# The last batch's q taken first and sorted by one-hots in its own layout: a linear attention with routed experts on one core

## The chip, the core and the metric

The kernel runs on one core of a Trainium2 chip. The metric is device time in microseconds (us), of one execution from its start to its end. The core has five engines with a queue of instructions each: TensorE (PE in the profile, PEld for its weight loads), VectorE (DVE), ScalarE (ACT), GpSimd (POOL) and SyncE (SP). An instruction waits for semaphores at the head of its queue, and what stands behind it waits too. SP issues the input transfers, POOL those of the experts' weights and of the output.

## The reference

The inputs are q, k and v of 8 batches, 8 heads, 576 positions and 64 features, one token number for each of the 4608 positions, and two weight matrices for each of 8 experts.

```
q_s = softmax(q) over the 64 features;  k_s = softmax(k) over the 576 positions
kv  = einsum('bhsd,bhse->bhde', k_s, v)
x   = einsum('bhsd,bhde->bhse', q_s, kv)         # as 4608 rows of 512
expert = token_ids * 2654435761 % 8
out[expert == e] = relu(x[expert == e] @ w1[e]) @ w2[e]     # w1: 512 x 1024, w2: 1024 x 512
```

## The kernel before, in words

The work has two stages. The first goes through the 8 batches (the loop at L750) and computes attention; while it does so it sorts the tokens of a batch by their expert and copies them into one tile xT, in which each expert has a stretch of 720 columns. The second goes through the experts: layer 1 (L692), ReLU, layer 2 (L717), and a store of the rows to their places (L733).

A batch of q, k or v lies in SBUF with 128 partitions: head parity times 64, and within a head 9 positions to a partition. There are two buffers each, so the loads of batch b + 2 are issued in batch b, once the tile is free (L776, L777); batches 0 and 1 are loaded ahead of the loop. q's load waits for exp_q, k's for exp_k, v's for cast_v of two batches before.

Within a batch b the order is written by hand, and each engine takes its own instructions in this order. ScalarE takes the exponentials of k (exp_k, L518); TensorE transposes the exponentials of q (transpose_q, L532); VectorE and ScalarE bring them to SBUF (qT_out, L544 to L547). TensorE then sorts the batch before: sort (L610) multiplies the attention's rows xn with a one-hot matrix, 384 columns for the first three tiles of 128 tokens and 192 for the other two, and ScalarE evicts to xs (L617). VectorE casts v to bf16 (cast_v, L526) and makes the one-hot matrix of a batch (one_hot, L601). kv (L557) multiplies k and v over 64 rows at a time, in pairs, into banks 6 and 7 of PSUM. kv_norm (L564, L568) divides by k's sum; qsum (L578, L582) has the sums of q's exponentials; attend (L586) multiplies, and VectorE scales the result to xn (L591). POOL copies 16 pieces of the sorted batch before to the experts' stretches (segments, L654).

Batch 0 has positions (L364 to L369), which gives each token its place, and segment_table (L373 and on); batch 2 has overflow (L402 and on).

At the seam of the stages the order on POOL is this. In batch 6 come 8 pieces of batch 5, then the four transfers of expert 0's w1 (weights1_half, L677, which wait until k of batch 7 has landed), then 8 more pieces. In batch 7 come the transfers of expert 1's w1 (weights1, L669) and expert 0's w2 (weights2, L683), then the pieces of batch 6 for experts 4 to 7. After the loop VectorE copies pieces for experts 0 to 3, and TensorE starts layer 1 of expert 0 on the first 320 columns, which need the pieces of batches 0 to 5 alone, with the sort of batch 7 between the second and the third of its four units (L821 to L825). Then expert 1 follows on its first 320 columns (L861). Layer 1 takes units of 256 hidden features (8 matmuls).

Of the kernel before, what the change touches and what calls it, by code (L numbers as in the profile page):

```python
# [4 lines left out]
F32 = mybir.dt.float32  # L5
# [159 lines left out]
def fused_kernel(nc, q, k, v, moe_token_ids, moe_w1, moe_w2, out):  # L165
# [4 lines left out]
    NC = 9  # L170
# [48 lines left out]
    selA = at("selA", [128, B * T, 128], BF16, vx0)  # L219
    selB = at("selB", [128, NG * TG, 2, B * T], BF16, vx0 + 10240)  # L220

    w1b, w2b, wreg = [], [], [qkv0, qkv0 + 18432, qkv0 + 36864, exp0]
    for i, o in enumerate(wreg):
        w1b.append(at("w1b%d" % i, [128, 4, F], BF16, o))
# [39 lines left out]
    dsf = at("dsf", [128, 4, NJ], F32)  # L264
    idxf = at("idxf", [128, B * T], F32)
    idx = at("idx", [128, B * T], I32)
    rk = [at("rk%d" % i, [128, 4], F32) for i in range(2)]
    rq = [at("rq%d" % i, [128, T, 8], F32) for i in range(2)]
    assert cur[0] <= 229000, cur[0]
# [8 lines left out]
    def dv(fn, R=(), W=(), P=()):  # L278
        em.op("dve", fn, R, W, P)
# [8 lines left out]
    b_q, b_k = [Buf(), Buf()], [Buf(), Buf()]  # L288
    b_v = [[Buf(), Buf()] for _ in range(2)]
    QKV = {"q": (qf, q), "k": (kf, k), "v": (vf, v)}  # L290

    def load_one(nm, b, p, js=range(2)):
        dst, src = QKV[nm]
        bb = [b_q[p]] if nm == "q" else [b_k[p]] if nm == "k" else [b_v[p][j] for j in js]
        js = slice(js[0], 4, 2 // len(js))
        em.dma("sync", "d_%s%d_%d" % (nm, p, js.start if js.step == 2 else 2), lambda e: e.dma_start(  # L296
            dst[p][:, js, :, :].rearrange("p h c d -> p h (c d)"),
            src[b].rearrange("(a h) (p c) d -> (h p) a (c d)", h=2, p=64)[:, js, :]), W=bb)

    load_one("q", 0, 0)  # L300
    em.dma("sync", "d_tok", lambda e: e.dma_start(
        tok64[:], moe_token_ids.rearrange("(b p c) -> p b c", b=B, p=64, c=NC)), P=[b_tok])
    b_vx = [[Buf(), Buf()] for _ in range(2)]
# [202 lines left out]
    def load(b, p):  # L506
        load_one("k", b, p)
        for js in ([(0,), (1,)] if b == B - 1 else [(0, 1)]):
            load_one("v", b, p, js)
# [11 lines left out]
            ACTF.Exp),  # L521
           R=[b_k[p]], W=[b_ek[p][j] for j in js])

    def cast_v(p, js=range(2)):
        o = slice(js[0], 4, 2 // len(js))
        dv(lambda e: e.tensor_copy(out=vx[p][:, o, :, 0:DH], in_=vf[p][:, o, :, :]), R=[b_v[p][j] for j in js],  # L526
           W=[b_vx[p][j] for j in js])

    def transpose_q(p):

# [17 lines left out]
                                   in_=PBH[:, 2048:2304].rearrange("p (j h x) -> p j h x", h=2, x=64)),  # L548
           R=[bk[2]], W=[b_qT[p][2]])

    def kv(p, js=range(2)):
        fns = []
        for j in js:
            for c in range(NC):
                for h2 in range(2):
                    r = slice(64 * h2, 64 * h2 + 64)
                    fns.append(lambda e, j=j, c=c, h2=h2, r=r: e.matmul(  # L557
                        PB[:, 6 + h2, 130 * j:130 * j + 130], ek[p][r, j, c, :, :].rearrange("p a d -> p (a d)"),
                        vx[p][r, j::2, c, :], start=(c == 0), stop=(c == NC - 1)))
        em.op("pe", fns, R=[b_ek[p][j] for j in js] + [b_vx[p][j] for j in js], W=[bk[6], bk[7]])  # L560

    def kv_norm(p):
        KV = PB[:, 6:8, 0:260].rearrange("p h (j a x) -> p j h a x", j=2, a=2)
        dv(lambda e: e.reciprocal(out=rk[p][:].rearrange("p (j h) -> p j h", h=2), in_=KV[:, :, :, 0, 64]),  # L564
           R=[bk[6], bk[7]], W=[b_rk[p]])
        for a in range(2):
            r = slice(64 * a, 64 * a + 64)
            dv(lambda e, a=a, r=r: e.tensor_tensor(  # L568
                out=kvn[p][r, :, a, :].rearrange("p (j h) x -> p j h x", h=2), in0=KV[r, :, :, a, 0:DH],
                in1=rk[p][r, :].rearrange("p (j h) -> p j h", h=2).unsqueeze(3).to_broadcast([64, 2, 2, DH]),  # L570
                op=ALU.mult), R=[bk[6], bk[7], b_rk[p]], W=([b_kvn[p]] if a == 0 else ()),
               P=(() if a == 0 else [b_kvn[p]]))

    def qt(p, t, j, h2):
        return qT[p][:, j, h2, 128 * t:128 * t + 128]
# [163 lines left out]
    def run(gen, n=2 * E):  # L739
        for _ in range(n):  # L740
            if next(gen, 0) == 0:
                break

    load(0, 0)
    load_one("q", 1, 1)
    load(1, 1)
    clear()
    exp_q(0, 0)
    exp_q(0, 1)
    for b in range(B):  # L750
        p = b % 2
        last = b == B - 1
        if last:
            transpose_q(p)
            exp_k(p, (0,))
            qT_out(p)
            exp_k(p, (1,))
            sort(1 - p, 0, 3)
            for j in range(2):
                cast_v(p, (j,))  # L760
                kv(p, (j,))
            sort(1 - p, 2, 0)
        else:
            exp_k(p)
            transpose_q(p)
            qT_out(p)
            if b > 0:
                sort(1 - p, 0, 3)
                sort(1 - p, 2, 0)
            if 1 < b < 6:  # L770
                load_segments(B - 2 + b // 4, "dve", 0, (b % 2,))
            cast_v(p)
            if b == 0:
                positions()
# [242 lines left out]
```

## Time and profile before

| what | us |
| --- | --- |
| median of three runs | 226.52 (226.42 to 226.86) |
| profiled execution | 226.57 |
| its span | 224.8 |
| PE busy | 192.4 (86%) |
| DVE busy | 124.2 (55%) |
| POOL busy | 117.8 (52%) |
| ACT busy | 106.8 (47%) |

The mean granted clock of TensorE was 0.982. In the page's slices each digit is the busy share of 5.62 us in tenths. A line of a chain or of a timeline begins with the start and the duration in us; "xN" is the number of instructions that it merges, and brackets at its end hold the idle time before it and what ended it. "DMA to landing" is the time from the start of an issue to the end of its transfer. A load of q, k or v moves 1152 KB.

### The profile page before, as it was taken

Reading aid. Unit: us, or ns where it says so; the run is one execution under the profiler, and the core shown is the slowest. Engines: PE = TensorE matmul, PEld = TensorE weight load, DVE = VectorE, ACT = ScalarE, POOL = GpSimd, SP = SyncE. Lnnn points to the kernel's source line nnn. Section 1 sums busy time; section 2 is a strip of 40 time slices with the busy share of each in tenths; the row PEclk is TensorE's granted clock in tenths of the full one; section 3 lists DMA queues with packets and bytes.
Section 4 is the critical chain, followed back from the end, with each engine's and each line's share of the span. In section 5 each row is a group of like instructions: output and inputs, shape, how many; then the busy total and the mean of one; then the engine's idle time right before and its main releaser. Section 6 shows DMA issues by size and latency. Waiting matters only on the chain.

```text
span 224.8 us, 4637 instructions
## 1 busy us (share of the span) xinstructions
PE 192.4 (86%) x1778; PEld 130.1 (58%) x1788; DVE 124.2 (55%) x274; ACT 106.8 (47%) x134; POOL 117.8 (52%) x227
## 2 busy tenths in 40 slices
PE   0439876777878689999999999999999999999990
PEld 0338656565666566774664855855845845846640
DVE  1589899999989964999912421421512412412220
ACT  3647787796898836673431422322322322322311
POOL 6410859992775994940018875615626525035053
PEclk9985999999999999999999999999999999999998
DMA  6999999999999999999955999999999797013033
GB/s 208 370 393 391 390 392 389 389 393 390 392 388 389 250 179 190 177 190 204 208 113 203 161 206 195 387 223 217 270 205 270 143 202 235 38 47 147 19 114 113
DMA packets 29791, 54.96 MB, mean 244 GB/s; under 512 B 2367, under 2 KB 11583, under 8 KB 29760
## 3 DMA queue, kind: packets, MB, share of 16 engines
q0 software_dynamic: 16544, 26.22, 55.5%
q1 hardware_dynamic: 13216, 28.35, 34.3%
q8 instruction: 16, 0.26, 0.5%
q14 instruction: 15, 0.12, 0.2%
HBM read 61.90 MB, written 10.49 MB: 322 GB/s over the span
## 4 chain that ended last, share of the span: by engine, by line
PE 67%; DVE 15%; DMA 12%; issue 2%; POOL 1%; SPq 1%; DVEq 0%; POOLq 0%
PE ps L717 30%; PE ps L692 28%; DMA vf<-in_v_dram 12%; DVE xn L591 7%; PE ps L610 5%; PE ps L557 3%; DVE vx L526 2%; DVE kvn L568 2%; DVE oneh L601 2%; PE ps L586 1%; POOL out_dram L733 1%; DVE qT L544 1%; PE ps L843 1%; SPq L296 0%; DVE rk L564 0%
## 5 line engine op out<-in xcount | busy, mean ns | idle before, releaser
L733 POOL DMA_INDIRECT out_dram<-yo,idx x40 | 39.5, 987 | 71.6 <-ACT yo L727 31.9
L717 PE MATMUL ps<-w2b,hT 128*128 128x512 bf16 x312 | 68.6, 379 | 0.4
L692 PE MATMUL ps<-xT,w1b 128*128 128x320 bf16 (+1 forms) x512 | 64.4, 286 | 0.7 <-DVE xn L591 0.7
L692 PEld LDWEIGHTS ps<-xT,w1b 128*128 128x128 bf16 x512 | 49.8, 98 | 14.9 <-DVE xn L591 1.1
L717 PEld LDWEIGHTS ps<-w2b,hT 128*128 128x128 bf16 x320 | 31.3, 98 | 36.2
L654 POOL COPY xT<-xs x112 | 42.2, 436 | 16.3 <-ACT xs L617 13.8
L699 ACT ACTIVATE hT<-ps 128x640 bf16<-128x640 f32 x41 | 28.9, 704 | 36.8 <-PE ps L692 36.5
L727 ACT ACTIVATE yo<-ps 128x512 f32<-128x512 f32 x26 | 15.5, 598 | 54.1 <-PE ps L717 54.1
L701 DVE TENSOR_SCALAR hT<-ps 128x640 bf16<-128x640 f32 x23 | 19.0, 825 | 30.2 <-PE ps L692 30.2
L729 DVE COPY yo<-ps 128x512 f32<-128x512 f32 x14 | 9.7, 692 | 44.0 <-PE ps L717 44.0
L610 PE MATMUL ps<-oneh,xn 128*128 128x384 bf16 (+1 forms) x160 | 23.5, 297 | 6.9 <-DVE xn L591 3.9
L591 DVE TENSOR_TENSOR xn<-ps,rq 128x1024 bf16<-128x1024 f32 (+1 forms) x24 | 23.6, 1040 | 1.8 <-PE ps L586 1.7
L610 PEld LDWEIGHTS ps<-oneh,xn 128*128 128x128 bf16 x160 | 14.4, 99 | 15.3 <-DVE xn L591 4.7
L617 ACT ACTIVATE xs<-ps 128x768 bf16<-128x768 f32 (+1 forms) x32 | 19.1, 648 | 8.7 <-PE ps L610 8.4
L512 ACT ACTIVATE eq<-qf 128x1152 bf16<-128x1152 f32 x16 | 17.7, 1159 | 8.2 <-DMA qf<-in_q_dram 8.2
L518 ACT ACTIVATE ek<-kf 128x2304 bf16<-128x2304 f32 (+1 forms) x9 | 17.2, 1909 | 4.3 <-DMA kf<-in_k_dram 4.2
L586 PE MATMUL ps<-kvn,qT 128*128 128x128 bf16 x160 | 11.3, 231 | 5.1 <-DVE kvn L568 5.1
L557 PE MATMUL ps<-vx,ek 64*128 64x130 bf16 x288 | 10.1, 218 | 4.5 <-DVE vx L526 4.3
L586 PEld LDWEIGHTS ps<-kvn,qT 128*128 128x128 bf16 x160 | 9.9, 104 | 5.7 <-DVE kvn L568 5.7
L683 POOL DMA_DIRECT2D w2b<-in_moe_w_dram x16 | 12.4, 801 | 0.0
L526 DVE CAST vx<-vf 128x2304 bf16<-128x2304 f32 (+1 forms) x9 | 11.8, 1323 | 1.0 <-DMA vf<-in_v_dram 1.0
L557 PEld LDWEIGHTS ps<-vx,ek 64*128 64x128 bf16 x288 | 8.5, 93 | 6.3 <-issue 3.7
(100 smaller groups left out, 135.1 us busy)
## 6 DMA issues: line engine op xcount, KB each, us to landing
qf<-in_q_dram SPq DMA_DIRECT2D x8, 1152.0 KB, 15.2
kf<-in_k_dram SPq DMA_DIRECT2D x8, 1152.0 KB, 15.5
w2b<-in_moe_w_dram POOLq DMA_DIRECT2D x16, 512.0 KB, 11.8
vf<-in_v_dram SPq DMA_DIRECT2D x7, 1152.0 KB, 15.4
w1b<-in_moe_w_dram POOLq DMA_DIRECT2D x14, 512.0 KB, 9.5
vf<-in_v_dram SPq DMA_DIRECT2D x2, 576.0 KB, 14.3
w1b<-in_moe_w_dram POOLq DMA_DIRECT2D x4, 256.0 KB, 5.6
out_dram<-yo,idx POOLq DMA_INDIRECT x40, 4.2
```

The source lines that it names most:

```text
L512: ac(lambda e: e.activation(eq[p][:, j, :, :, :].rearrange("p c a d -> p a c d"), qf[p][:, j::2, :, :], ACTF.Exp), R=[b_q[p]], W=[b_eq[p][j]])
L557: fns.append(lambda e, j=j, c=c, h2=h2, r=r: e.matmul(PB[:, 6 + h2, 130 * j:130 * j + 130], ek[p][r, j, c, :, :].rearrange("p a d -> p (a ...
L586: em.op("pe", [lambda e, i=i, j=j, h2=h2: e.matmul(PB[:, bank + i, 256 * j + 128 * h2:256 * j + 128 * h2 + 128], qt(p, t0 + i, j, h2), kvn ...
L591: dv(lambda e: e.tensor_tensor(out=xn[p][:, t0:t0 + n, :].rearrange("p t (g x) -> p (t g) x", x=DH), in0=PB[:, bank:bank + n, :].rearrange ...
L610: em.op("pe", [lambda e, g=g, i=i, k=k, n=n: e.matmul(PB[:, bank + (k if g == 0 else 2), (0 if g == 0 else GW[1] * k):(GW[0] if g == 0 els ...
L617: ac(lambda e, g=g, src=src: e.activation(xs[p][:, c0:c0 + 2, XO[g]:XO[g] + GW[g]], src, ACTF.Copy), R=bs, P=b_xs[p][c0:c0 + 2])
L654: return e.tensor_copy(out=xT[:, :, bass.ds(do, SEG[g])], in_=xs[p][:, :, XO[g]:XO[g] + GW[g] + SEG[g]][:, :, bass.ds(so, SEG[g])])
L692: em.op("pe", [lambda e, d=d, k=k: e.matmul(cut(PB[:, u + k, 0:H2]), w1b[s][:, d, 128 * (f + k):128 * (f + k) + 128], cut(rhs(d)), start=( ...
L699: ac(lambda e: e.activation(o, i, ACTF.Relu), R=bk[u:u + 2], W=[b_hT[hp][hf][f // 2]])
L701: dv(lambda e: e.tensor_scalar(out=o, in0=i, scalar1=0.0, scalar2=None, op0=ALU.max), R=bk[u:u + 2], W=[b_hT[hp][hf][f // 2]])
L717: em.op("pe", [lambda e, fc=fc: e.matmul(PB[:, u, :], hT[hp][:, fc, 128 * t:128 * t + 128], w2b[s][:, fc, :], start=(fc == 0), stop=(fc == ...
L733: em.dma("pool", "d_o%d" % y, lambda e: e.indirect_dma_start(out=out[:, :], out_offset=IndirectOffsetOnAxis(ap=idx[:, 5 * ee + t:5 * ee + ...
```

## The change

q of batch 7 is loaded as the first of all inputs, into a tile qe of its own, and no longer in batch 5. The new tiles lie where the hidden layers hT stand later. Ahead of batch 0 ScalarE takes its exponentials (exp_early), and VectorE sums, inverts and multiplies, so that q is normalised in its own layout (norm_early, tile en). Behind positions, two small transfers on POOL and two copies spread the places of batch 7's tokens over both halves of the partitions (places_early); behind segment_table VectorE makes nine one-hot matrices, one for each of the 9 positions of a partition (one_hot_early). In batches 2 to 5 TensorE sorts a quarter each of this q between the two sorts of the batch before, into banks 6 and 7, and ScalarE evicts it to qs (sort_early).

The loop now ends with batch 6. Batch 7 stands behind it: no transposes, no qsum, no attend, no sort. Its v is cast in halves, one on ScalarE; kv runs in halves, the first into banks 0 and 1; kv_norm_half normalises each; attend_sorted multiplies kv by the sorted q and yields sorted columns, which are evicted straight to xs. The order of POOL's transfers and copies is kept. The two first units of layer 1 stand behind attend_sorted. The former exponentials of batch 7's q and its one-hots leave batch 6.

```
+    qe = at("qe", [128, 4, NC, DH], F32, hT0)
+    oe = at("oe", [128, 6 * GW[0] + 3 * GW[1]], BF16, hT0)
+    en = at("en", [128, 2, NC, 2, DH], BF16, hT0 + 10240)
+    qs = at("qs", [128, 4, S], BF16, hT0 + 14848)
...
-    load_one("q", 0, 0)
+    em.dma("sync", "d_qe", lambda e: e.dma_start(
+        qe[:].rearrange("p h c d -> p h (c d)"),
+        q[B - 1].rearrange("(a h) (p c) d -> (h p) a (c d)", h=2, p=64)), W=[b_qe])
...
-    def cast_v(p, js=range(2)):
+    def cast_v(p, js=range(2), onact=False):
...
+        R, W = [b_v[p][j] for j in js], [b_vx[p][j] for j in js]
+        if onact:
+            ac(lambda e: e.activation(vx[p][:, o, :, 0:DH], vf[p][:, o, :, :], ACTF.Copy), R=R, W=W)
+        else:
+            dv(lambda e: e.tensor_copy(out=vx[p][:, o, :, 0:DH], in_=vf[p][:, o, :, :]), R=R, W=W)
+
+    def exp_early():
+        ac(lambda e: e.activation(qe[:], qe[:], ACTF.Exp), W=[b_qe])
+
+    def norm_early():
+        dv(lambda e: e.tensor_reduce(out=dn[:], in_=qe[:], axis=AX.X, op=ALU.add), R=[b_qe], W=[b_dn])
+        dv(lambda e: e.reciprocal(out=dn[:], in_=dn[:]), W=[b_dn])
+        for j in range(2):
+            dv(lambda e, j=j: e.tensor_tensor(
+                out=en[:, j, :, :, :].rearrange("p c a d -> p a c d"), in0=qe[:, j::2, :, :],
+                in1=dn[:, j::2, :].unsqueeze(3).to_broadcast([128, 2, NC, DH]), op=ALU.mult),
+               R=[b_qe, b_dn], P=[b_en])
+
...
+    def places_early():
+        for h in range(2):
+            r, o = slice(64 * h, 64 * h + 64), slice(64 - 64 * h, 128 - 64 * h)
+            src = pos[r, 2 * B - 2:2 * B, :].rearrange("p g t -> p (g t)")
+            dv(lambda e, h=h, r=r, src=src: e.tensor_copy(out=pd[r, h, :], in_=src), R=[b_pos], P=[b_pd])
+            em.dma("pool", "d_pd", lambda e, h=h, o=o, src=src: e.dma_start(pd[o, h, :], src), R=[b_pos], P=[b_pd])
...
+    def one_hot_early():
+        for c in range(NC):
+            g = c // 6
+            dv(lambda e, c=c, g=g: e.tensor_scalar(
+                out=oe[:, col_early(c):col_early(c) + GW[g]], in0=col16[:, 0:GW[g]],
+                scalar1=pd[:, c % 2, c // 2:c // 2 + 1], scalar2=None, op0=ALU.is_equal),
+               R=[b_pd, bc["col16"]], W=([b_qe] if c == 0 else ()), P=[b_oe])
+
+    def sort_early(j, g):
+        cs_ = range(6) if g == 0 else range(6, NC)
+        em.op("pe", [lambda e, c=c, h=h: e.matmul(
+            PB[:, 6 + h, 0:GW[g]], en[64 * h:64 * h + 64, j, c, :, :].rearrange("p a d -> p (a d)"),
+            oe[64 * h:64 * h + 64, col_early(c):col_early(c) + GW[g]], start=(c == cs_[0]), stop=(c == cs_[-1]))
+            for c in cs_ for h in range(2)], R=[b_en, b_oe], W=bk[6:8])
+        ac(lambda e: e.activation(qs[:, 2 * j:2 * j + 2, GW[0] * g:GW[0] * g + GW[g]], PB[:, 6:8, 0:GW[g]], ACTF.Copy),
+           R=bk[6:8], P=[b_qs])
+
+    def attend_sorted(p, j, bank, key):
+        for g, bs in ((0, bk[bank:bank + 2]), (1, bk[bank + 2:bank + 3])):
+            em.op("pe", [lambda e, g=g, h=h: e.matmul(
+                PB[:, bank + (h if g == 0 else 2), (0 if g == 0 else GW[1] * h):(GW[0] if g == 0 else GW[1] * (h + 1))],
+                kvn[p][:, 2 * j + h, :, :].rearrange("p a x -> p (a x)"), qs[:, 2 * j + h, GW[0] * g:GW[0] * g + GW[g]],
+                start=True, stop=True) for h in range(2)], R=[b_qs, b_kvl[j]], W=bs)
+            src = PB[:, bank:bank + 2, 0:GW[0]] if g == 0 else \
+                PB[:, bank + 2, 0:2 * GW[1]].rearrange("p (k x) -> p k x", k=2)
+            dst = xs[p][:, 2 * j:2 * j + 2, XO[g]:XO[g] + GW[g]]
+            if key == "act":
+                ac(lambda e, src=src, dst=dst: e.activation(dst, src, ACTF.Copy), R=bs, P=b_xs[p][2 * j:2 * j + 2])
+            else:
+                dv(lambda e, src=src, dst=dst: e.tensor_copy(out=dst, in_=src), R=bs, P=b_xs[p][2 * j:2 * j + 2])
...
-    def kv(p, js=range(2)):
+    def kv(p, js=range(2), u=6):
...
+    def kv_norm_half(p, j, u):
+        KV = PB[:, u:u + 2, 130 * j:130 * j + 130].rearrange("p h (a x) -> p h a x", a=2)
+        rh = rk[p][:, 2 * j:2 * j + 2]
+        dv(lambda e: e.reciprocal(out=rh, in_=KV[:, :, 0, 64]), R=bk[u:u + 2], W=[b_rkl[j]])
+        for a in range(2):
+            r = slice(64 * a, 64 * a + 64)
+            dv(lambda e, a=a, r=r: e.tensor_tensor(
+                out=kvn[p][r, 2 * j:2 * j + 2, a, :], in0=KV[r, :, a, 0:DH],
+                in1=rh[r, :].unsqueeze(2).to_broadcast([64, 2, DH]), op=ALU.mult),
+               R=bk[u:u + 2] + [b_rkl[j]], P=[b_kvl[j]])
...
+    load_one("q", 0, 0)
     load(0, 0)
     load_one("q", 1, 1)
     load(1, 1)
     clear()
+    exp_early()
+    norm_early()
     exp_q(0, 0)
     exp_q(0, 1)
-    for b in range(B):
+    for b in range(B - 1):
         p = b % 2
-        last = b == B - 1
-        if last:
-            transpose_q(p)
-            exp_k(p, (0,))
-            qT_out(p)
-            exp_k(p, (1,))
+        exp_k(p)
+        transpose_q(p)
+        qT_out(p)
+        if b > 0:
             sort(1 - p, 0, 3)
-            for j in range(2):
-                cast_v(p, (j,))
-                kv(p, (j,))
+            if 1 < b < 6:
+                sort_early((b - 2) // 2, b % 2)
             sort(1 - p, 2, 0)
-        else:
-            exp_k(p)
-            transpose_q(p)
-            qT_out(p)
-            if b > 0:
-                sort(1 - p, 0, 3)
-                sort(1 - p, 2, 0)
-            if 1 < b < 6:
-                load_segments(B - 2 + b // 4, "dve", 0, (b % 2,))
-            cast_v(p)
-            if b == 0:
-                positions()
-            if b + 2 < B:
-                load_one("q", b + 2, p)
-                load(b + 2, p)
-            if b > 0:
-                one_hot(b if b < 4 else b + 1)
+        if 1 < b < 6:
+            load_segments(B - 2 + b // 4, "dve", 0, (b % 2,))
+        cast_v(p)
+        if b == 0:
+            positions()
+            places_early()
+        if b + 2 < B - 1:
+            load_one("q", b + 2, p)
+        if b + 2 < B:
+            load(b + 2, p)
+        if 0 < b < 6:
+            one_hot(b if b < 4 else b + 1)
+        if b < B - 2:
             exp_q(1 - p, 0)
             exp_q(1 - p, 1)
-            kv(p)
+        kv(p)
         kv_norm(p)
         qsum(p)
         if b == 0:
@@ -793,12 +866,6 @@
             weights1_half(0, 0, 0, R=[b_k[1]])
             weights1_half(0, 0, 1)
             run(sg)
-        elif last:
-            weights1(1, 1)
-            weights2(0, 0)
-            for x in (b - 1, b):
-                load_segments(x, "pool", 1)
-            run(segments(b - 1, "pool", 1))
         elif b > 0:
             load_segments(b - 1, "pool")
             run(segments(b - 1))
@@ -808,6 +875,7 @@
         if b == 0:
             segment_table()
             widths()
+            one_hot_early()
         if b == 2:
             overflow()
         if b == 3:
@@ -815,14 +883,35 @@
         if b == 2:
             load_widths()
 
+    p = 1
+    b_kvl = [Buf(b_kvn[p]), Buf(b_kvn[p])]
+    b_rkl = [Buf(b_rk[p]), Buf(b_rk[p])]
+    exp_k(p, (0,))
+    exp_k(p, (1,))
+    weights1(1, 1)
+    weights2(0, 0)
+    for x in (B - 2, B - 1):
+        load_segments(x, "pool", 1)
+    cast_v(p, (0,), True)
+    kv(p, (0,), 0)
+    sort(1 - p, 0, 3)
+    cast_v(p, (1,))
+    kv(p, (1,), 6)
+    kv_norm_half(p, 0, 0)
+    kv_norm_half(p, 1, 6)
+    sort(1 - p, 2, 0)
+    run(segments(B - 2, "pool", 1))
+    attend_sorted(p, 0, 3, "act")
+    attend_sorted(p, 1, 0, "dve")
+    for i, bs in enumerate(([b_qe, b_oe], [b_en, b_qs])):
+        b_hT[i] = [[Buf(*bs) for _ in range(FC // 2)] for _ in range(2)]
+    b_kvn[p], b_rk[p] = Buf(*b_kvl), Buf(*b_rkl)
 
     for s, bs in ((2, [b_k[1]] + b_v[1]), (3, b_eq[0] + b_eq[1] + b_ek[0] + b_ek[1])):
         b_w1[s], b_w2[s] = [Buf(*bs), Buf(*bs)], Buf(*bs)
+    for f in range(0, FC // 2, 2):
+        l1(0, f, 0, 6 - 3 * f, True)
     run(segments(B - 2, "dve", 0))
-    for f in range(0, FC // 2, 2):
-        l1(0, f, 0, 3 * f, True)
-    sort(p, 0, 3)
-    sort(p, 2, 0)
     run(segments(B - 1, "dve", 0))
     run(segments(B - 1, "pool", 1))
     weights2(1, 1)
```

More of the change, by code (lines that the diff above doesn't have):

```diff
@@ L266, in fused_kernel @@
     idx = at("idx", [128, B * T], I32)
+    dn = at("dn", [128, 4, NC], F32)
+    pd = at("pd", [128, 2, 2 * TG], F32)
     rk = [at("rk%d" % i, [128, 4], F32) for i in range(2)]
@@ L290, in fused_kernel @@
     QKV = {"q": (qf, q), "k": (kf, k), "v": (vf, v)}
+    b_qe, b_oe, b_en, b_qs, b_dn, b_pd = (Buf() for _ in range(6))
     def load_one(nm, b, p, js=range(2)):
@@ L522, in exp_k @@
            R=[b_k[p]], W=[b_ek[p][j] for j in js])
-    def cast_v(p, js=range(2)):
+    def cast_v(p, js=range(2), onact=False):
         o = slice(js[0], 4, 2 // len(js))
-        dv(lambda e: e.tensor_copy(out=vx[p][:, o, :, 0:DH], in_=vf[p][:, o, :, :]), R=[b_v[p][j] for j in js],
-           W=[b_vx[p][j] for j in js])
+        R, W = [b_v[p][j] for j in js], [b_vx[p][j] for j in js]
[3 more added lines that the diff above has]
+            dv(lambda e: e.tensor_copy(out=vx[p][:, o, :, 0:DH], in_=vf[p][:, o, :, :]), R=R, W=W)
@@ new lines, in places_early, with col_early @@
+    def places_early():
[4 more added lines that the diff above has]
+            em.dma("pool", "d_pd", lambda e, h=h, o=o, src=src: e.dma_start(pd[o, h, :], src), R=[b_pos], P=[b_pd])
+    def col_early(c):
+        return GW[0] * c if c < 6 else 6 * GW[0] + GW[1] * (c - 6)
@@ L557, in kv @@
                     fns.append(lambda e, j=j, c=c, h2=h2, r=r: e.matmul(
-                        PB[:, 6 + h2, 130 * j:130 * j + 130], ek[p][r, j, c, :, :].rearrange("p a d -> p (a d)"),
+                        PB[:, u + h2, 130 * j:130 * j + 130], ek[p][r, j, c, :, :].rearrange("p a d -> p (a d)"),
                         vx[p][r, j::2, c, :], start=(c == 0), stop=(c == NC - 1)))
-        em.op("pe", fns, R=[b_ek[p][j] for j in js] + [b_vx[p][j] for j in js], W=[bk[6], bk[7]])
+        em.op("pe", fns, R=[b_ek[p][j] for j in js] + [b_vx[p][j] for j in js], W=bk[u:u + 2])
     def kv_norm(p):
```

## The prediction

> **What bounds the kernel now.** I read the page's slices first, then the chain that ended last, then the timeline around the hand-over, then the landings of the first weights.
>
> ```profile
> PE   0439876777878689999999999999999999999990
> DVE  1589899999989964999912421421512412412220
> DMA  6999999999999999999955999999999797013033
> ```
>
> A slice is 5.62 us. Up to slice 13 (79 us) the inputs flow and VectorE is at eight or nine tenths; from slice 15 TensorE is full to the end. So there are two stages, and the change works at their seam.
>
> ```profile
> 42.05 0.60 DVE qT L544
> 42.65 0.20 DVE qT L547
> 42.85 1.41 DVE vx L526
> 44.26 0.05 issue
> 44.30 1.23 PE ps L557 x36
> ...
> 65.14 2.37 DVE xn L591 x2
> 67.51 0.05 issue
> 67.56 2.78 PE ps L610 x20
> 70.34 1.16 PE ps L557 x36
> ```
>
> These are pieces of the chain. After 32.16 us it holds no DMA: it alternates between VectorE and TensorE with gaps of a few hundredths. The transfers run at their own pace: the exponential of k starts on a landing at 38.20, 65.33 and 74.37 us, 9.04 us a batch, 3.01 us a load. Computing a batch takes 8.2 us (L557 at 53.90, 62.09, 70.27), and at batch 6 it has barely caught up (v lands near 68.4, its cast starts at 68.81). So **a microsecond put on VectorE early in the first stage stays** unless a wait absorbs it.
>
> ```profile
> 71.49 3.20 POOL L654 COPY xT<-xs  x8 [2.67 <-ACT xs L617]
> 74.65 2.76 POOL L677 DMA_DIRECT2D w1b<-in_moe_w_dram  x4
> 77.40 3.36 POOL L654 COPY xT<-xs  x8
> 80.71 1.22 POOL L669 DMA_DIRECT2D w1b<-in_moe_w_dram  x2
> ...
> 85.62 2.77 PE L610 MATMUL ps<-oneh,xn 128*128 128x384 bf16 x20
> ...
> 88.23 12.58 PE L692 MATMUL ps<-xT,w1b 128*128 128x320 bf16 x96
> ```
>
> The timeline at the seam. On POOL the copies of batch 5 start when ScalarE has evicted its sort, and expert 0's and 1's weights are issued between and behind these copies. The end is TensorE: sort of batch 7 until 88.39, then layer 1 without a gap.
>
> ```profile
> L669 POOL DMA_DIRECT2D w1b<-in_moe_w_dram x2: 610/615/620, 80.7 to 81.3; - x2
> DMA to landing us min/median/max: 5.8/6.8/7.8
> ```
>
> Expert 1's w1: the second half, issued at 81.3, lands 7.8 later, at 89.1 us. Its first matmuls come two units of 1.05 us after 88.39, at 90.5. **The slack is 1.4 us**: the weights are nearly as late as TensorE.
>
> **Part by part.** Batch 5's evicted sort (71.24 us now, the end of L617's fourth copy) is my reference point; call its delay the lag.
>
> *Loads.* q of batch 7 goes first, so every load up to v of batch 6 lands one slot, 3.0 us, later; k and v of batch 7 land as before (74.4, about 77), since their place in the byte stream is the same. On SP no other order changes. A load of v waits for the cast two batches earlier; the tightest is v of batch 7 behind cast(5), at 62.0 + lag, and its slot opens at 74.3: no bubble under a lag of some 10.
>
> *exp_early*: 2304 elements on ScalarE, 2.12 us as L518, from 6.7 to 8.8 while ScalarE would wait for q of batch 0 (9.9): free.
>
> *norm_early*, on VectorE behind L362 (done 11.52) and ahead of batch 0. The reduce of 2304 elements: L402 takes 208 ns for 64 and L373 546 for 384, 1.056 ns an element, so 2.57 us; from the strided L367 (673 for 384), in proportion, 4.0 at most; by the slope alone 2.43 at least. I take 2.57, which has both rows of the same operation with it. Reciprocal of 36: 0.38, from L582 (408 ns for 40). Two multiplies of 1152: L477 (1920, 2153 ns) and L452 (384, 560) give 1.037 ns an element, 1.36 each. With three gaps 5.75 us: 11.5 to 17.3. Then qT 0.69 and 0.28 and the cast 1.36: cast(0) ends at 19.6, not 14.28. Lag 5.3, of which the later load would have explained 3.0.
>
> The Trainium skill speaks against this step ("VectorE: DVE Perf Modes", Rules for kernel authors): a tensor_reduce on the hot path runs at one element a cycle, and it advises restructuring. By its clock of 0.96 GHz the reduce would be an estimated 2.4 us against the rows' 2.57.
>
> *places_early*: two copies of 64x6 at about 0.18 (L342: 180 ns for 64x32): 0.35. Its two transfers wait on POOL for the positions; behind them stand only the segment table's operations, which wait longer anyway. *one_hot_early*: nine, at the spacing of L601 (five in 1.13 us): 2.05. They follow the segment table near 28.4; the transfer, with the 5.7 us of the token load, lands between 27 and 29.1, so up to 0.8 more; I take nothing. Lag 5.3 + 0.35 + 2.05 = 7.75 at batch 1. Batch 2's cast waited 0.40 for its load; that wait absorbs its part: 7.35.
>
> *sort_early*, on TensorE between the two sorts of batches 2 to 5: twelve matmuls of 384 columns (batches 2, 4) or six of 192 (3, 5), over 64 rows, in pairs. L557 has the same pairs: 36x130 columns in 1.21 us, 3.87 a ns; L610, with 128 rows, 6144 in 2.78 us, 2.21 a ns. By the first 1.19 and 0.30 us, by the second 2.09 and 0.52; I take the first, whose pattern is the same. Batch 2: TensorE had 0.4 us before the second sort and 0.57 behind kv, so 0.26 stays (1.16). Batch 3: hidden behind overflow's 1.7 us on VectorE. Batch 4: the second sort started at 52.43 behind qT, and the first ended at 51.26: 0.02 stays (0.92). Batch 5: the sort runs straight into kv, so all 0.30 (0.52). Lag 7.35 + 0.26 + 0.02 + 0.30 = **7.9**, with the upper values 9.95. ScalarE's evictions (0.81 or 0.49, as L617) and the banks 6 and 7 they release are ready before kv needs them.
>
> Switching between 64 and 128 rows shows no gap above 0.1 us now (sort to kv at 70.3, kv to qsum at 71.4). The Trainium skill ("TensorEngine Tiling (Array Packing)", Key Properties) says that a change of tiling mode drains TensorE; the trace prices that at nothing.
>
> *Removed in batches 5 to 7*: exp_q, one_hot(7), transposes and qT_out. In batch 6 VectorE without one_hot gains nothing: TensorE's sort and kv ended 0.3 us later than it.
>
> *The last batch on TensorE.* Now from batch 6's xn (76.29) to the end of sort(7) (88.39) are 12.1 us, with two layer 1 units, 2.1, inside. After: half a cast 0.95, half a kv 0.70, a normalisation half 0.8 (0.18 + two of 0.29, from L564 and L568), sort(6)'s second part 1.48 beside the other half, two attends of 1152 columns 0.52 each, at L610's rate, and gaps: 4.3. The path to layer 1 shortens by 12.1 - 2.1 - 4.3 = **5.7**. The half cast on ScalarE (1.16, as L518's halves) is over before sort(6). Against a lag of 7.9 this alone ends 2.2 later.
>
> *The weights.* POOL's copies of batch 5 start 7.9 later, so everything behind them does: expert 1's w1 is issued at 88.6 and lands at 89.1 + 7.9 = 97.0. Layer 1 of expert 0 (four units, 4.2 us) starts at 88.5 and is done at 92.7; TensorE then stands until 97.0, where it began expert 1 at 90.5: **6.5 later**. Were the queue quicker because the inputs are over, it gains at most about 1. From there order and durations are those of before, and the next weights are shifted alike; w2 of expert 0 landed at 95.3 for 100.86, so has room. The shorter TensorE path is thus hidden behind a transfer.
>
> Sum: the profiled execution took 226.57 us (span 224.8, 1.8 around it), 0.05 over the median of 226.52: 226.57 + 6.5 = 233.1.
>
> **Rivals.**
> - *TensorE's own path decides*: the weights land in time, because POOL's copies or the queue without inputs are quicker. Then lag 7.9 - 5.7 = 2.2, 228.8. For it: only 1.4 us separated them. Against: the same POOL order, two copies' blocks of 3.2 and 3.4 and 5.6 us a MB.
> - *VectorE absorbs the early work*: the lag is only the load's 3.0. Then w1 of expert 1 lands at 92.1: +1.6, 228.2. Against: the chain without a DMA from 32 us on.
> - *Faster*: the shorter last batch wins. It takes a lag under 5.7 and weights that land with it; at 3.0, 5.7 - 3.0 = 2.7 less, 223.9. For it: 2.8 us of sort and all of qsum and attend really leave TensorE. Against: VectorE's slices, and the 1.4 us.
> - *Worse*: the upper sort_early, reduce and transfer: lag above 10.5, over 235.8.
>
> **How the numbers follow.** Forecast 0.68 (lag 7 to 10.5: 231 to 235.8), TensorE's path 0.12, absorbed 0.06, faster 0.09, worse 0.05. The range 228.6 to 235.8 holds the first two. About 0.2% (0.45 us) is what the measurement tells from no change: faster 0.09, same 0.02, slower 0.89.
>
> **What would show it.** norm_early's rows between 11.5 and 17.3; cast(0) near 18.3 to 19.6; no wait of VectorE on DMA in batches 1 to 6; the end of batch 5's evictions near 79; L677 near 82.5; a gap on TensorE of 3 to 5 us inside L692, at some 93 to 97, with no cover from ScalarE or VectorE. I am wrong if that gap is missing, if the reduce is far from 2.6 us, or if the evictions come by 75.

## The result and the profile after

The kernel after takes 235.22 us (234.69 to 236.02, four runs) against 226.69 (226.42 to 227.07, four runs): a ratio of 1.0378, interval [1.0338, 1.0418], 8.5 us slower, where 6.5 were forecast. The profiled execution took 235.69 us (span 233.8, clock 0.987), so against the profiled one of before the span grew by 9.0. Of all executions in this document one, of 233.58 us, stands more than 1.5% above the fastest of its kernel; it counts as a slow one and is left out where it occurs.

The page's slices of the kernel after (busy tenths; a slice is now 5.85 us):

```profile
PE   0235758787887886599999999999999999999990
DVE  1699999798998788999902241331322421422220
DMA  6999999999999069999971599999999799103023
```

TensorE fills up only from slice 17 (99 us), and it has a hole in slices 15 and 16. The DMA row has a hole too, in slice 13 (76 to 82 us): the inputs are over, and the weights have not been issued.

The timeline of VectorE in the kernel after, at the start:

```profile
11.44 2.54 DVE L546 TENSOR_REDUCE dn<-qe 128x36 f32<-128x2304 f32 x1
14.01 0.38 DVE L547 RECIPROCAL dn<-dn 128x36 f32<-128x36 f32 x1
14.43 2.62 DVE L549 TENSOR_TENSOR en<-qe,dn 128x1152 bf16<-128x1152 f32 x2
```

norm_early stands between 11.4 and 17.0: the reduce, the reciprocal and two multiplies. The cast of batch 0 follows at 17.77 and takes 1.35, so it ends at 19.1 (19.6 forecast). The same kernel's timeline of POOL at the seam (L731 is the old L654, L754 the old L677, L746 the old L669):

```profile
79.46 3.20 POOL L731 COPY xT<-xs  x8 [2.69 <-ACT xs L694]
82.60 2.73 POOL L754 DMA_DIRECT2D w1b<-in_moe_w_dram  x4
85.32 2.36 POOL L731 COPY xT<-xs  x8
87.64 1.22 POOL L746 DMA_DIRECT2D w1b<-in_moe_w_dram  x2
```

The copies of batch 5 begin at 79.46, not 71.49: a lag of 7.97. And TensorE behind them:

```profile
88.56 2.34 PE L769 MATMUL ps<-xT,w1b 128*128 128x320 bf16 x16
92.77 2.35 PE L769 MATMUL ps<-xT,w1b 128*128 128x320 bf16 x16 [1.87 <-DMA w1b<-in_moe_w_dram]
97.76 12.09 PE L769 MATMUL ps<-xT,w1b 128*128 128x320 bf16 x80 [2.65 <-DMA w1b<-in_moe_w_dram]
109.90 8.58 PE L794 MATMUL ps<-w2b,hT 128*128 128x512 bf16 x39
```

The brackets are the reading. TensorE stands twice for weights, first for the second half of expert 0's w1, then for expert 1's. Expert 1 starts at 97.76 instead of 90.5 (+7.2), layer 2 at 109.90 instead of 100.86 (+9.04), and from there the shift stays at 9.0 to the end. The last pieces of this kernel's chain name the same:

```profile
88.24 9.47 DMA w1b<-in_moe_w_dram
...
97.76 12.09 PE ps L769 x80
```

So expert 1's transfer is on the chain for 9.47 us. The pieces ahead of it, from 79.46 on, are POOL's copies and issues, one behind the other. One line is not explained by it: the ten units behind the wait (80 matmuls) took 12.09 us, where ten units at full clock are 10.4. The windows of the kernel after (us, then the busy time of PE, PEld, DVE, ACT and POOL, each with its number of instructions, then PEclk, DMA share, GB/s):

```profile
98.00:100.00 2.00, 2.00 (x10) 1.09 (x9) 1.79 (x7) 0.08 (x1) 2.00 (x4) 0.50 1.24 207
100.00:102.00 2.00, 2.00 (x11) 1.22 (x10) 1.90 (x4) 0.80 (x2) 1.42 (x3) 0.65 1.24 206
102.00:104.00 2.00, 2.00 (x17) 1.44 (x15) 1.72 (x11) 1.23 (x3) 0.00 (x0) 1.00 1.25 207
```

Ten and eleven matmuls in two microseconds, then seventeen: the granted clock was 0.50 from 98.0 to 101.4.

### The profile page after: what moved, and what is told of

The parts are those of the page before. It is cut to its first block, busy times and chain, and to the rows that moved or that the text cites. A ratio compares the mean times of both kernels' runs of the same rounds, so it can differ in the third digit from the quotient of the medians.

```text
span 233.8 us, 4581 instructions
## 1 busy us (share of the span) xinstructions
PE 193.8 (83%) x1744; PEld 128.1 (55%) x1754; DVE 130.1 (56%) x282; ACT 107.5 (46%) x135; POOL 117.2 (50%) x229
## 4 chain that ended last, share of the span: by engine, by line
PE 63%; DVE 19%; DMA 7%; POOL 4%; issue 4%; POOLq 1%; ACT 0%; SPq 0%; DVEq 0%; ACTq 0%
PE ps L794 27%; PE ps L769 26%; DVE xn L668 7%; PE ps L687 5%; DMA w1b<-in_moe_w_dram 4%; PE ps L623 3%; DMA tok<-in_moe_token_ids_dram 2%; DVE kvn L634 2%; POOL xT L731 2%; POOL out_dram L810 2%; PE ps L663 1%; DVE vx L540 1%; DVE dn L546 1%; DVE oneh L678 1%; DVE qT L610 1%
## 5 line engine op out<-in xcount | busy, mean ns | idle before, releaser
L769 PE MATMUL ps<-xT,w1b 128*128 128x320 bf16 (+1 forms) x512 | 66.1, 290 | 4.5 <-DMA w1b<-in_moe_w_dram 4.5
L731 POOL COPY xT<-xs x112 | 39.9, 412 | 16.5 <-ACT xs L694 14.1
L687 PE MATMUL ps<-oneh,xn 128*128 128x384 bf16 (+1 forms) x140 | 20.5, 295 | 7.6 <-DVE qT L610 3.8
L694 ACT ACTIVATE xs<-ps 128x768 bf16<-128x768 f32 (+1 forms) x28 | 16.7, 648 | 12.2 <-PE ps L687 11.9
L668 DVE TENSOR_TENSOR xn<-ps,rq 128x1024 bf16<-128x1024 f32 (+1 forms) x21 | 20.7, 1039 | 1.7 <-PE ps L663 1.7
L687 PEld LDWEIGHTS ps<-oneh,xn 128*128 128x128 bf16 x140 | 12.2, 98 | 15.4 <-DVE qT L610 4.7
L522 ACT ACTIVATE eq<-qf 128x1152 bf16<-128x1152 f32 x14 | 15.5, 1162 | 4.3 <-DMA qf<-in_q_dram 4.3
L663 PE MATMUL ps<-kvn,qT 128*128 128x128 bf16 x140 | 10.1, 232 | 4.3 <-DVE kvn L634 4.3
L598 PE MATMUL ps<-ident,eq 128*128 128x128 bf16 x126 | 10.0, 242 | 2.9 <-ACT eq L522 2.0
L663 PEld LDWEIGHTS ps<-kvn,qT 128*128 128x128 bf16 x140 | 8.8, 104 | 4.9 <-DVE kvn L634 4.9
```

The lines of the kernel that those rows point to most:

```text
L663: em.op("pe", [lambda e, i=i, j=j, h2=h2: e.matmul(PB[:, bank + i, 256 * j + 128 * h2:256 * j + 128 * h2 + 128], qt(p, t0 + i, j, h2), kvn ...
L668: dv(lambda e: e.tensor_tensor(out=xn[p][:, t0:t0 + n, :].rearrange("p t (g x) -> p (t g) x", x=DH), in0=PB[:, bank:bank + n, :].rearrange ...
L687: em.op("pe", [lambda e, g=g, i=i, k=k, n=n: e.matmul(PB[:, bank + (k if g == 0 else 2), (0 if g == 0 else GW[1] * k):(GW[0] if g == 0 els ...
L694: ac(lambda e, g=g, src=src: e.activation(xs[p][:, c0:c0 + 2, XO[g]:XO[g] + GW[g]], src, ACTF.Copy), R=bs, P=b_xs[p][c0:c0 + 2])
L731: return e.tensor_copy(out=xT[:, :, bass.ds(do, SEG[g])], in_=xs[p][:, :, XO[g]:XO[g] + GW[g] + SEG[g]][:, :, bass.ds(so, SEG[g])])
L769: em.op("pe", [lambda e, d=d, k=k: e.matmul(cut(PB[:, u + k, 0:H2]), w1b[s][:, d, 128 * (f + k):128 * (f + k) + 128], cut(rhs(d)), start=( ...
```

## The experiments

The theory: the lag of 8 us pushes expert 1's w1 past the moment at which TensorE wants it, so the end is set by the issue of the weights; the lag itself is 3 us of load order, some 4 of VectorE's early work and the rest early sorts. Rivals: the weights wait only hides TensorE's own path (then nothing is won by earlier weights), or the load order alone makes the lag.

**Weights issued ahead.** Expert 0's w1 before the 16 copies of batch 5, expert 1's w1 behind the first eight of them.

```
-            load_segments(b - 1, "pool")
-            sg = segments(b - 1)
-            run(sg, 8)
             weights1_half(0, 0, 0, R=[b_k[1]])
             weights1_half(0, 0, 1)
+            load_segments(b - 1, "pool")
+            sg = segments(b - 1)
+            run(sg, 8)
+            weights1(1, 1)
             run(sg)
+            weights2(0, 0)
...
-    weights1(1, 1)
-    weights2(0, 0)
```

> The changed kernel with one thing moved: on POOL the four transfers of expert 0's w1 stand ahead of the 16 copies of batch 5, and expert 1's w1 behind the first 8 of them. Theory (the weights set the end): POOL stood idle for 2.7 us ahead of these copies, so the transfers cost the copies nothing; expert 1's w1 lands near 91, layer 1 of expert 0 starts at 88.6 as in the changed kernel and runs without a wait, expert 1 starts at 92.9 instead of 97.8, TensorE's clock is granted in full, and the time is about 229 us. Rival A (VectorE's early work reaches the end through TensorE's own order, and the weights only happen to be late): the time stays at 234 to 235.5. Rival B (the later loads do it): the same, 234 to 235.5.

Measured: 231.28 us (230.91 to 232.53), ratio 1.0198 [1.0161, 1.0236]. TensorE's wait for weights is gone and 3.9 us with it, so the wait was real. But the time is some 2.3 over the expectation, and the timeline of this kernel shows on what:

```profile
84.84 3.16 DVE L540 CAST vx<-vf 128x1152 bf16<-128x1152 f32 x1
...
88.06 0.69 PE L623 MATMUL ps<-vx,ek 64*128 64x130 bf16 x18 [2.20 <-DVE vx L540]
```

The half cast took 3.16 us, where the kernel after has 1.00 for it at 84.18. Beside it POOL issues expert 1's w1 until 85.9 and then copies until 88.8; in the kernel after POOL only issued transfers beside the cast. Removing one wait made another of 2.2 us. POOL's copies by themselves are not the reason for the 3.16: in the kernel with both edits, further down, the same half cast ran inside POOL's copies and took 0.75.

**No early work on VectorE.** norm_early and one_hot_early left out (so the rows of batch 7 are not computed), and POOL fills their two tiles with zeros instead; the load order and the early sorts stay.

```
-    norm_early()
+    gp(lambda e: e.memset(en[:].rearrange("p a c b d -> p (a c b d)").bitcast(F32), 0.0), P=[b_en])
+    gp(lambda e: e.memset(oe[:].bitcast(F32), 0.0), W=[b_qe], P=[b_oe])
...
-            one_hot_early()
```

> The changed kernel without VectorE's early work: the sum, the reciprocal, the two multiplies and the nine one-hots of batch 7 are left out, and POOL fills both tiles with zeros while it is idle, so the rows of batch 7 are not computed; all that follows runs with the same shapes. Theory: the copies of batch 5 start near 74.8 instead of 79.5, expert 1's w1 lands near 92.5, and TensorE, ready near 88, waits 4 us for it and then has a lower clock: 228 to 231. Rival A (the lag alone counts, without the weights): 226.6 + 3.3 - 5.7 = 224 to 225. Rival B (the later loads alone): no change, 235.

Measured: 229.55, 231.31 and 231.88 us, within the theory's 228 to 231 or up to 0.9 over it; the median of the three is 1.019 of the 226.90 that the kernel before took beside them. The copies of batch 5 start at 75.61, 4.12 us after those of before, where the whole change has 7.97, so VectorE's early work is 3.85 of the lag. This kernel's TensorE:

```profile
88.67 2.35 PE L769 MATMUL ps<-xT,w1b 128*128 128x320 bf16 x16 [1.63 <-DMA w1b<-in_moe_w_dram]
93.81 6.38 PE L769 MATMUL ps<-xT,w1b 128*128 128x320 bf16 x46 [2.79 <-DMA w1b<-in_moe_w_dram]
```

The lag is halved, and the waits are as long as in the kernel after (1.87 and 2.65): TensorE and the weights both came forward by the same 4 us. The three executions had mean clocks of 0.996, 0.987 and 0.988; 3.41 us at half clock would be 0.0075 of the span, so the two that took 1.8 and 2.3 us longer may each have lost one such stretch more. The profiled one, the fastest, shows a clock of 1.00 behind the same waits.

**Both edits together.** As the two diffs above.

> Both edits before at once; the rows of batch 7 are again not computed. Theory: the weights land near 88.5, TensorE's shorter last batch shows at last, 224 to 225.5, faster than the kernel before. Rival A: the same 224 to 225, no less than with VectorE's work left out alone. Rival B: 235.

Measured: 228.44 us (227.64 to 230.56, seven runs), ratio 1.0067 [1.0031, 1.0102]. A miss by 3: the expected gain over before did not come. This kernel's TensorE:

```profile
86.82 3.43 PE L769 MATMUL ps<-xT,w1b 128*128 128x320 bf16 x24 [0.66 <-DVE xs L593]
92.09 10.41 PE L769 MATMUL ps<-xT,w1b 128*128 128x320 bf16 x80 [1.83 <-DMA w1b<-in_moe_w_dram]
```

Expert 1's w1 stood behind eight copies still and landed at 92.0, so expert 1 began 1.6 us after that of before (90.5). The half cast of batch 7's v in this kernel, and POOL beside it:

```profile
78.40 3.79 POOL L731 COPY xT<-xs  x8 [0.97 <-ACT ek L528]
80.72 0.75 DVE L540 CAST vx<-vf 128x1152 bf16<-128x1152 f32 x1
```

The cast is faster than in the kernel after, though POOL copied all the while; here it is POOL's eight copies that are slower, 3.79 against the 3.20 of the kernel after.

**The load order alone.** The kernel before, with q of batch 7 loaded first into a tile of its own and used from there; nothing is sorted early.

```
-    load_one("q", 0, 0)
+    em.dma("sync", "d_qe", lambda e: e.dma_start(
+        qe[:].rearrange("p h c d -> p h (c d)"),
+        q[B - 1].rearrange("(a h) (p c) d -> (h p) a (c d)", h=2, p=64)), W=[b_qe])
...
+    load_one("q", 0, 0)
     load(0, 0)
...
-            if b + 2 < B:
+            if b + 2 < B - 1:
                 load_one("q", b + 2, p)
+            if b + 2 < B:
                 load(b + 2, p)
...
-            exp_q(1 - p, 0)
-            exp_q(1 - p, 1)
+            exp_q(1 - p, 0, b == B - 2)
+            exp_q(1 - p, 1, b == B - 2)
```

> The kernel before with the order of the loads alone: q of batch 7 goes first, into a tile of its own, and its exponentials are taken from there in batch 6. Theory: every load but the last two comes 3.0 us later, VectorE's slack takes 0.4 of it, and the copies of batch 5, the weights and the last sort all move by 2.6 to 3: 229.0 to 229.8, with no wait for weights of over 1 us. Rival A: 226.7, the loads have no part. Rival B: 234 to 235, all of it.

Measured: 229.74 us (229.11 to 229.95), ratio 1.0115 [1.0091, 1.0139]: as expected, one load slot. Its copies of batch 5 start at 74.75, 3.26 after those of before, and its weights with them:

```profile
74.75 3.21 POOL L659 COPY xT<-xs  x8 [2.66 <-ACT xs L622]
77.89 2.76 POOL L682 DMA_DIRECT2D w1b<-in_moe_w_dram  x4
```

So the lag is 3.26 of loads, 0.86 that goes with the rest of the change (no run separates the early sorts in it), 3.85 of VectorE: 7.97.

**TensorE kept busy in its two waits.** Matmuls whose results nobody reads, nine in the first wait and thirteen in the second.

```
         l1(0, f, 0, 6 - 3 * f, True)
+    keep_busy(9)
...
+        if i == 2:
+            keep_busy(13)
         l1(ee, f, 0, (6, 3, 0, 6, 4, 2)[i], True)
```

> The changed kernel with matmuls of no use in TensorE's two waits for expert 0's and expert 1's weights: nine of 128x512 ahead of the third unit of layer 1, thirteen ahead of the fifth, into a bank that nobody reads. The weights land as before. Theory (the two waits, 1.9 and 2.7 us, cost the clock as well: it was granted at 0.50 from 98 to about 101.4 us, and two units took 1.8 longer): the granted clock stays at 1.00, and the time falls from about 235.2 by 1 to 1.8, to 233.4 to 234.2. Rival (the lower clock has another cause, or costs nothing): 234.8 to 235.6.

Measured: 234.4 us (233.31 to 235.05), ratio 1.0330 [1.0297, 1.0362]; the median lies between theory and rival, 0.8 under the kernel after, with overlapping ranges, so the time does not decide. The profile is clearer. TensorE of this kernel:

```profile
95.97 2.97 PE L916 MATMUL ps<-w1b 128*128 128x512 bf16 x13
98.82 10.41 PE L769 MATMUL ps<-xT,w1b 128*128 128x320 bf16 x80
```

The ten units take 10.41 again, not 12.09: in this execution, where TensorE did not stand at the seam, the clock did not drop there. It lost about 1.0 earlier, where it had half clock from 30.1 to 33.5 us. The execution of the highest mean clock (0.997) took 233.31.

**Weights ahead and the second half cast on ScalarE.** Against the 2.2 us of the first experiment.

```
-    sort(1 - p, 0, 3)
-    cast_v(p, (1,))
+    cast_v(p, (1,), True)
+    sort(1 - p, 0, 3)
     kv(p, (1,), 6)
```

> As weights_ahead, with the second half of batch 7's v cast on ScalarE as well. In weights_ahead this cast took 3.2 us on VectorE beside POOL's copies, against 1.0 in the changed kernel, and TensorE stood 2.2 us for it. Theory (VectorE and POOL shut each other out): without it layer 1 starts 2 to 3 us sooner, 228.3 to 229.3. Rival (the weights or the lag set the end in weights_ahead): 231, as there.

Measured: 231.41 us (230.72 to 232.2), ratio 1.0212 [1.0182, 1.0242]. The wait for the cast is gone and TensorE's layer 1 runs without a gap from 90.59, yet the time is that of the first experiment. In the profiled execution the lag grew early. Its TensorE, and the windows there:

```profile
31.68 2.27 PE L687 MATMUL ps<-oneh,xn 128*128 128x384 bf16 x10 [3.91 <-DVE qT L610]
```

```profile
32.00:36.00 4.00, 4.00 (x53) 2.96 (x51) 2.29 (x7) 2.65 (x4) 1.79 (x3) 0.57 1.05 390
```

TensorE stood 3.91 us there for VectorE (the nine one-hots; 2.92 in the kernel after), and the clock was halved behind it, from 32.2 to 35.6: the sort took 2.27 and not 1.48, kv 2.00 and not 1.21, together 1.6 of lag. So layer 2 starts at 105.18, only 0.79 ahead of the first experiment (105.97). That lead goes at the row table: TensorE stands 0.76 us for VectorE's selA ahead of the table's product at 118.56, a wait that the first experiment does not have, and the next layer 2 starts at 120.01 against 119.86. How often the early halving comes, one profile can't say.

**Tokens first, one-hots on POOL.** The token load ahead of q of batch 7, and one_hot_early on POOL.

```
+    em.dma("sync", "d_tok", lambda e: e.dma_start(
+        tok64[:], moe_token_ids.rearrange("(b p c) -> p b c", b=B, p=64, c=NC)), P=[b_tok])
     em.dma("sync", "d_qe", lambda e: e.dma_start(
...
-            dv(lambda e, c=c, g=g: e.tensor_scalar(
+            gp(lambda e, c=c, g=g: e.tensor_scalar(
...
             places_early()
+            one_hot_early()
...
             widths()
-            one_hot_early()
```

> The changed kernel with the token numbers loaded ahead of q of batch 7, so that VectorE's first chain is over before that q has its exponentials, and with the nine one-hots of batch 7 on POOL. Order of the weights as in the changed kernel. Theory: the early sum and multiplies then end before v of batch 0 lands (15.9 us), the lag falls from 8.0 to the 3 to 3.5 of the later loads, and the time is that of no_early_vector, 229.5 to 231.5. Rival (the work itself costs, wherever it stands): 233 to 235.

Measured: 237.77 us (237.17 to 238.98), ratio 1.0509 [1.0477, 1.0542], a clear miss, above the rival as well. The early chain did end sooner (cast of batch 0 at 16.57, not 17.77), but POOL of this kernel shows:

```profile
26.25 10.52 POOL L567 TENSOR_SCALAR oe<-col,pd 128x384 bf16<-128x384 f16 x9 [4.64 <-DVE xn L668]
```

Nine one-hots take 10.52 us there, 2.36 on VectorE, and what stands behind them on POOL holds VectorE's cast of batch 2 for 4.57.

**All four edits** (this one, the weights and the cast):

> Token numbers first, one-hots on POOL, expert 0's and expert 1's w1 ahead of the copies of batch 5, and both halves of batch 7's v cast on ScalarE. Theory: the weights flow from 76 us on without a gap and land at 83.5 and 88.7, layer 1 starts near 84 and does not wait over 0.5 us for expert 1, against 90.5 in the kernel before: 225 to 226, a little faster than the kernel before at 226.9. Rival (the later loads bound it, as in order_of_loads_alone): 228 to 230.

Measured: 232.7 us (231.44 to 234.13), ratio 1.0276 [1.0242, 1.0310]. A miss with the same row: the one-hots took 10.87 us on POOL. In the profiled execution the clock was also halved from 42.2 to 52.5 us.

**The ceiling.** No early work on VectorE (the rows of batch 7 are not computed), both w1 ahead of all copies, both half casts on ScalarE.

```
             weights1_half(0, 0, 1)
+            weights1(1, 1)
             load_segments(b - 1, "pool")
             run(segments(b - 1))
+            weights2(0, 0)
```

> What the change could bring if VectorE's early work cost nothing: as no_early_vector (the rows of batch 7 are not computed, POOL writes zeros instead), with expert 0's and expert 1's w1 both ahead of the copies of batch 5 and both halves of batch 7's v cast on ScalarE. Theory: the lag is that of the later loads and of sort_early, 3.2 to 4.1; the weights flow from 76 us without a gap, expert 1's lands by 89; layer 1 starts near 84.5 and does not wait: 225 to 226 against 226.8 before. Rival (the later loads give all of it back): 227.5 to 229.

Measured: 228.67 us (228.17 to 230.03), ratio 1.0095 [1.0066, 1.0124]. Here TensorE starts expert 1 earlier than before did (89.86 against 90.5) and layer 2 as well (100.17 against 100.86), and the kernel still ends later. What its TensorE waits for then:

```profile
115.00 1.61 PE L930 MATMUL ps<-selB,selA 128*128 128x80 bf16 x40 [2.21 <-DVE selA L504]
```

A third engine is late next. VectorE's sixteen copies, which before made in two blocks with room between them, run in one piece beside POOL's copies (86.34 to 95.27, 8.72 us of copying against 4.64), so the table of the output's rows starts at 95.38 instead of 92.58, and TensorE waits for it. What stretches the copies is not shown: in the first experiment sixteen in one piece, also beside POOL's, took 4.99.

**Tokens first and weights ahead**, all rows computed, one-hots on VectorE, both half casts on ScalarE:

> The changed kernel, all computed, with the token numbers loaded first, both w1 ahead of the copies of batch 5 and both halves of batch 7's v cast on ScalarE; the one-hots stay on VectorE. Theory: lag 6.5 to 7, layer 1 of expert 0 starts near 87.5 and does not wait for weights, 227.5 to 229 where no early drop of the clock comes in, up to 1.5 more where it does. Rival (the moved weights only shift the copies of batch 5, which TensorE then waits for): 231 to 233.

Measured: 231.94 us (231.45 to 232.61), ratio 1.0237 [1.0213, 1.0261], a miss; the rival's range holds it, but not its mechanism, as TensorE did not wait for the copies of batch 5. No wait for weights, but 0.45 for VectorE's later copies and 1.74 for its table, as in the ceiling, and half clock from 30.1 to 33.5 us.

**The kernel before with the weights ahead.**

> The kernel before with both w1 ahead of the copies of batch 5, nothing else. Theory (there TensorE's own order sets the end, and the weights have 1.4 us to spare): no change, 226.4 to 227.2. Rival (the weights set the end before the change as well): 1 to 1.4 us faster, 225.4 to 225.8.

Measured: 226.48 us (225.73 to 227.09, twelve runs), ratio 0.9991 [0.9978, 1.0005]: no change, so in the kernel before the weights had slack and TensorE's own order set the end.

**The ceiling with the table later.** The product that makes the row table three layer 2 tiles later on TensorE, and the stores of those tiles behind it.

```
-                if ee == 1:
-                    index_table()
...
                 for t in range(T):
+                    if ee == 1 and t == 3:
+                        index_table()
```

> As the kernel called ceiling (q of batch 7 is not summed, normalised or turned into one-hots, so the rows of batch 7 are not computed; both experts' w1 are issued ahead of the copies; the halves of v are cast on ScalarE), and the matrix product that makes the index table on TensorE stands behind three tiles of expert 1's layer 2 instead of ahead of them, with the stores of those tiles behind it. In ceiling TensorE stood 2.21 us ahead of that product, for VectorE's selA at 114.95. Theory (VectorE's late chain, copies and then the index table, gives TensorE's gain back): the three tiles take 3.1 us, so the wait goes and the time is 228.67 - 2.2 = 226.5, 226.0 to 227.0. Rival (the wait only hid something else that is as late, the weights of expert 2 or the stores): the wait of TensorE comes back further on and the time stays at 228.2 to 229.0.

Measured: 228.41 us (228.28 to 230.04), ratio 1.0083 [1.0057, 1.0110]. The wait of 2.21 went, and at 122.70 this kernel is 0.47 ahead of before at the same unit (123.17), and still at 138.82 (139.29). Then, in the eight units from 138.82 on, it loses the lead:

```profile
142.86 1.10 PE L769 MATMUL ps<-xT,w1b 128*128 128x0 bf16 x8 [0.77 <-issue]
144.91 4.20 PE L769 MATMUL ps<-xT,w1b 128*128 128x0 bf16 x32 [0.95 <-ACT hT L776]
```

Before took 8.22 us for these eight units, this kernel 10.1, because the evictions of the hidden layer came late. What held those evictions the profile does not name, so this part stays open. The rival's time was right; its mechanism, a wait that comes back further on, is seen, its cause is not.

## Why the prediction was right, and where it was short

*The lag.* Forecast 7.9, measured 7.97. Its parts hold within half a microsecond, and that the total is closer than they are is luck: loads 3.26 (3.0 a slot); VectorE's early work 3.85 beyond them, where the sum had 5.3 - 3.0 + 0.35 + 2.05 - 0.40 = 4.3; 0.86 for what is left, where the early sorts had 0.58. (On the way the sum 5.3 + 0.35 + 2.05 was put at 7.75; it is 7.70, and 7.9 stays.) The rows are right one by one: reduce 2.54 (2.57), reciprocal 0.38, multiplies 2.62 (2.72), the nine one-hots 2.36 (2.05), sort_early 1.15 (1.19) and 0.42 (0.30). The price by L557's pairs, not by L610, was the right choice.

*The last batch.* Forecast to shorten TensorE's path by 5.7; layer 1 began at 88.56 (88.5 forecast). That gain exists and is hidden, as the step said.

*The weights.* Forecast: w1 of expert 1 issued at 88.6, landing at 97.0. Measured: its second half was issued at 88.2, a microsecond sooner than the sum had it (81.3 + 7.9), as POOL's second eight copies took 2.36 and not 3.36; and it landed at 97.7, since 9.5 us passed and not 7.8. Without the inputs beside it the transfer was not quicker; why it took longer no run shows. Expert 0's second half was late too, which the step did not see (it had all four units done at 92.7); so the one gap of 4.3 us that the sum had came as two, of 1.87 and 2.65. The first does not set the end, because TensorE stands for expert 1 anyway. The experiment with weights ahead shows that the wait was worth 3.9 us of the time and not all of it: beneath it lay the wait of 2.2 for VectorE's half cast.

*The step that failed* is the sentence "From there order and durations are those of before". Behind the waits the clock was 0.50 for 3.41 us, which made ten units 12.09 and not 10.4: 1.7 of the 2.5 us by which the profiled execution exceeded the sum. The rest is the landing, 0.7. That the standing is the cause is supported by the experiment that kept TensorE busy (10.41). But standing does not always cost it: the kernel without VectorE's early work stood as long (1.63 and 2.79) and kept its clock in the profiled execution, while the one with the one-hots on POOL (1.73 and 2.91) had half clock again, and 11.78 for the ten units.

The Trainium skill ("TensorE: Matmul & The Clock Gate", What's actually happening) puts the clock at half after an idle window of about 3.4 us, counted in free-running windows of 3413 ns. The length of the drop agrees, 3.41 us here. The condition differs: no single wait here was 3.4 us, and the window before the drop, 94.6 to 98.0, held 0.5 us of work at its start and 0.24 at its end. The traces give the phase of such windows, and it fits. In the kernel after the clock is halved from 98.0 and once more, behind the last matmul, from 231.1: 39 times 3.413 us apart. In the kernel without VectorE's early work the only halving begins at 225.84; 39 times 3.413 us before it lies 92.7, in the middle of the second wait (91.0 to 93.8), so the stretches on both sides of it held 1.70 and 2.33 us of work, and no halving followed. With the one-hots on POOL the stretch before the halving at 99.2 held 1.08. No threshold comes out of this: with the weights ahead a stretch with 1.48 us (84.0 to 87.4) was not followed by a halving, and one with 1.94 (43.0 to 46.4) was.

*The rivals.* "TensorE's own path decides", at 228.8, would have come if the weights had landed in time. With the weights ahead it came to 231.28, so that rival lacked the wait for VectorE's cast. "Faster", at 223.9, needed a lag of 3.0 and early weights. The ceiling had nearly these, and ended at 228.67: behind the weights stands VectorE, with its copies and the row table. No version that was run beats the kernel before.

## What to carry to other kernels

A gain on one engine at a hand-over counts only up to the next thing that is late there, so list the slack of every engine and of the weights at the seam; here it was 1.4 us for the weights, and VectorE's row table was late next. Work that is added early on an engine without slack comes back at the end, less what it shares with another delay: VectorE's early rows sum to some 8.3 us, and 3.85 came back beyond the 3.26 of the later loads. And price a new wait of TensorE of some microseconds with a possible drop of its clock behind it, not at the wait alone.

## What the runs showed of the hardware

A halved clock lasted 3.41 us each time that one was seen alone, at other places in other executions: at 98.0 in the kernel after, from 30.1 in two experiments, from 32.2 in a third. VectorE's half cast of v took 1.00 us while POOL issued transfers, 3.16 while POOL issued and went on to copy, and 0.75 inside POOL's copies, which then took 3.79 instead of 3.20. The Trainium skill ("SBUF — State Buffer", Who interferes with whom) has GpSimd and VectorE share a pair of ports under an exclusive lock in such copies and casts. That one of the two is slower each time would fit, but no run tried the cast by itself, and none shows what decides which of them pays. VectorE's sixteen copies at the seam took 4.64 in before, 4.99 with the weights ahead, 7.50 in the kernel after and 8.72 in the ceiling, each time beside POOL's copies. POOL took 10.52 us for nine one-hots, 1.17 each, VectorE 0.26 each. Between sorts over 128 rows and an early sort over 64 rows no gap above 0.1 us appeared.
